# Issuing three stores and one small load from GpSimd instead of SyncE in a two-part state-space kernel

## The chip, the cores and the metric

The kernel runs on one core of a Trainium2 chip. The metric is the time of one execution on the device in microseconds (us); of several runs the median counts. The core has five engines that run side by side, each through its own list of instructions in order: TensorE (PE in the profile, with its weight loads as PEld), VectorE (DVE), ScalarE (ACT), GpSimd (POOL) and SyncE (SP). Data moves between the main memory (DRAM) and the on-chip memory by transfers (DMAs). A transfer is issued by an instruction of one of the engines; an instruction that waits, for data or for a transfer, holds up everything behind it on its engine.

## The reference

Two independent parts, over 2048 steps and 640 channels, are computed and set side by side. Part A is a diagonal linear recurrence with complex state (S5), part B a short convolution and a long one (H3). Cut to what matters:

```python
def part_a(x, Lambda, Bmat, Cmat, log_dt, Dskip):
    Lam_bar = exp(exp(log_dt) * Lambda)
    h[t] = Lam_bar * h[t - 1] + B_bar @ x[t]
    return 2 * real(Cmat @ h) + x * Dskip

def part_b(q, k, v, shift_k, ssm_k, ssm_D):
    k_shift = sum(k_pad[:, t:t + S] * shift_k[:, 3 - t] for t in range(4))
    kv = k_shift * v
    y = irfft(rfft(kv, 2 * S) * rfft(ssm_k, 2 * S))[:S]
    return q * (y + kv * ssm_D)

out = concatenate([part_a(...), part_b(...)], axis=-1)
```

Inputs and output are bf16. "D's row" below is `Dskip`, the 640 numbers that part A multiplies x by.

## The kernel before

All data lies in one on-chip array (`arena`), cut into named parts. `P.add` registers one operation with the engines that may run it, what it reads and what it writes; there are 815 of them. A hand-written table, `ORDER`, lists them as number, engine letter (T TensorE, V VectorE, A ScalarE, G GpSimd, S SyncE) and accumulator bank. `Program.emit` (L122) goes down the table and puts each operation at the end of its engine's list. It makes an operation wait for all that it depends on where that ran on another engine or is a transfer. So the table alone sets what stands behind what on each engine, and nearly all transfers stand in SyncE's list.

Part B takes k and v in five blocks of 128 channels (d = 0 to 4). For each block:

- `load_kv` (L811) loads k and v turned by the transfer (channels on partitions), L814. There is one buffer for k, so the k of the next block can only be issued when the last tap of this block has read it. For v there are three.
- `conv` (L827) makes four taps (`cm`, a multiplication by one weight per channel; its instructions are recorded under L205 on VectorE and L206 on ScalarE), three additions (`ca`, L840), and the product with v (`cx`, L841), which stays in v's buffer.
- `plane` (L843) stores the product, 128 x 2048, as 128 rows of `kv_rows`, a scratch tensor in DRAM (`pl`, L847). 

The stored rows come back in another layout by `relay` (L850): eight transfers per half (`rl`, L857), which need the rows of blocks 0 to 2 for the first half. TensorE then runs the long convolution in stages (`s1` L876 and L881, `s2` L900, `r2` L951, `r1` L972). What they leave in the accumulator is moved out by ScalarE or VectorE at L886, L913, L956 and L990. The filter `ssm_k` is loaded per half by four transfers (`load_h`, L807), to which VectorE adds the direct term (L809).

Part A builds its state by matmuls (L581, L602), a scan over the coarse steps (`coarse`, L656, whose products L679 and sums L690 run on VectorE) and a way back down (L728). Its last stage, `project` (L732), has 16 pieces: load 128 rows of x (L736), multiply them by D's row (`xd`, L737), project the state by TensorE (`C`, recorded under L225, or L229 where `wide` splits a matmul in two), add both (`ev_C`, L754) and store (L765). D's row is loaded once, spread over 128 partitions, by `ld_Dr` (L372). The x rows of the turned kind (L547) and C (`load_C`, L556) are loaded by SyncE too.

In the table of before, the three stores of blocks 0 to 2 (operations 388, 399 and 410) and D's row (91) are SyncE's. The first store stands behind the load of block 2's k, the second behind the load of C's imaginary part and ahead of block 3's k, the third behind the first relay. D's row stands behind the second half's `ssm_k`.

Of the kernel before, what the change touches and what calls it, by code (L numbers as in the profile page):

```python
# [20 lines left out]
PACT, PDVE, PPOOL, PPE, PSP = "A", "V", "G", "T", "S"  # L21
# [177 lines left out]
class Ctx:  # L199
# [9 lines left out]
    def v(self, name, lo=0, n=None):  # L209
        at, size = LAY.at[name]  # L210
        n = size - lo if n is None else n
        assert lo + n <= size
        return self.arena[:, at + lo:at + lo + n]
# [18 lines left out]
def bc(ap, shape):  # L232
    return ap.to_broadcast(shape)
# [124 lines left out]
def params(c):  # L358

    P, nc, v, f = c.P, c.nc, c.v, c.f  # L360
    V, G, A = PDVE, PPOOL, PACT
    lam_re, lam_im, ldt_in, dsk_in = c.ins["A_Lambda_re"], c.ins["A_Lambda_im"], c.ins["A_log_dt"], c.ins["A_Dskip"]
# [3 lines left out]
    for k, src in enumerate((lam_re, lam_im, ldt_in)):  # L366
        rows = pr[10 * k:10 * k + 10, :]
        P.add("ld_par", {PSP: .1, PACT: .1}, lambda e, rows=rows, src=src: e.dma_start(
            out=rows.rearrange("p (a b) -> p a b", a=2), in_=bass.AP(src.tensor, 0, [[64, 10], [0, 2], [1, 64]])),
            outs=[tk[:, k:k + 1]], ins=[pr], nbytes=2560)  # L370
    c.DR = v("DR")
    P.add("ld_Dr", {PSP: .1}, lambda e: e.dma_start(out=c.DR, in_=bass.AP(dsk_in.tensor, 0, [[0, 128], [1, 640]])), outs=[c.DR],  # L372
          nbytes=128 * 1280)
    PV = v("PV").bitcast(f32)
    g = P.group(1)
# [11 lines left out]
    for i, n in enumerate((1, 2, 4, 8, 16)):  # L387
        P.add("rn", {A: .2}, lambda e, i=i, n=n: e.activation(out=rn[:, i, :], in_=rho, func=FN.Exp, scale=float(n)),
              outs=[rn[:, i, :]], ins=[rho])
# [17 lines left out]
    for i in range(1, 4):  # L407
        P.add("fn", {G: .2}, lambda e, i=i: e.tensor_tensor(out=fn[:, i, :], in0=fn[:, i - 1, :], in1=fn[:, i - 1, :], op=ALU.add),
              outs=[fn[:, i, :]], ins=[fn[:, i - 1, :]])
    P.add("ph", {G: .4}, lambda e: e.tensor_tensor(  # L410
        out=ph.rearrange("p (x m) -> p x m", m=2), in0=bc(fn.rearrange("p n j -> p (n j)").rearrange("p (x o) -> p x o", o=1), [128, 40, 2]),
# [5 lines left out]
        out=al3, in0=al3, in1=bc(rn[:, 0:4, :].rearrange("p n j -> p (n j)").rearrange("p (x o) -> p x o", o=1), [128, 40, 2]), op=ALU.mult),  # L417
        outs=[al], ins=[al, rn[:, 0:4, :]])
# [4 lines left out]
    for lo, mi, val in ((0, 0, 1.0), (0, 1, 0.0), (64, 0, 0.0), (64, 1, 1.0)):  # L423
# [17 lines left out]
          outs=[t3(ga)[:, :, 0]], ins=[t3(ma)[:, :, 0], t3(mb)[:, :, 1]])  # L441
    P.add("ga1", {V: .12}, lambda e: e.tensor_tensor(out=t3(ga)[:, :, 1], in0=t3(mb)[:, :, 0], in1=t3(ma)[:, :, 1], op=ALU.subtract),
          outs=[t3(ga)[:, :, 1]], ins=[t3(mb)[:, :, 0], t3(ma)[:, :, 1]])
# [26 lines left out]
    for x in range(2):  # L470
        ps, pc, jx = phs[:, 640 * x:640 * x + 640], phc[:, 640 * x:640 * x + 640], Fi[:, 5 * x:5 * x + 5]
        P.add("sph", {G: 1.2}, lambda e, ps=ps, jx=jx: e.tensor_tensor(
            out=ps.rearrange("p (j s) -> p j s", j=5), in0=bc(s16.rearrange("p (o s) -> p o s", o=1), [128, 5, 128]),
            in1=bc(jx.rearrange("p (j o) -> p j o", o=1), [128, 5, 128]), op=ALU.mult), outs=[ps], ins=[s16, jx])
        P.add("cph", {G: 1.2}, lambda e, ps=ps, pc=pc: e.tensor_tensor(out=pc, in0=ps, in1=bc(c30, [128, 640]), op=ALU.add),
              outs=[pc], ins=[ps, c30])
# [291 lines left out]
class PartB:  # L768
# [74 lines left out]
    def plane(self, d):  # L843

        c, P = self.c, self.c.P
        vt, tok = c.v("VT", 2048 * (d % 3), 2048), c.tok[:, d:d + 1]
        P.add(f"pl{d}", {PSP: 1.6}, lambda e: e.dma_start(out=c.kvdram[128 * d:128 * d + 128, :], in_=vt), outs=[tok], ins=[vt],  # L847
              nbytes=128 * 4096)

    def relay(self, hf):  # L850
# [162 lines left out]
def build(c):  # L1013
# [5 lines left out]
    setup(c)  # L1019
    tables_G(c)  # L1020
    params(c)
    b.load_small()
    for k in range(3):
# [74 lines left out]
def plain_order(P):  # L1098
# [16 lines left out]


ORDER = (
# [40 lines left out]
)  # L1158


# [68 lines left out]
```

## Time and profile before

| what | value |
|---|---|
| runs of the program | 187.35, 187.96 and 188.18 us; median 187.96 |
| span of the profiled execution | 187.3 us, 7665 instructions |
| TensorE clock granted | full in all 40 slices |
| DMA: bytes moved | 30.15 MB, 161 GB/s on average |
| DMA: time of the queue that SyncE issues to (q1) | 86.7% of 16 engines' span |
| DMA: time of the other queues together (q8, q10, q14) | 1.8% |

The profile gives no total for the profiled execution apart from its span, 187.3 us; the fastest of the three runs took 187.35, so hardly anything of a run lies outside the span. A transfer shows up twice: as an instruction of the issuing engine's queue (SPq), whose duration is the issue, and by its landing, the time from the issue to when the data is there. GpSimd issues no transfer in this kernel.

### The profile page before, as it was taken

Reading aid. Unit: us, or ns where it says so; the run is one execution under the profiler, and the core shown is the slowest. Engines: PE = TensorE matmul, PEld = TensorE weight load, DVE = VectorE, ACT = ScalarE, POOL = GpSimd, SP = SyncE. Lnnn points to the kernel's source line nnn. Section 1 sums busy time; section 2 is a strip of 40 time slices with the busy share of each in tenths; the row PEclk is TensorE's granted clock in tenths of the full one; section 3 lists DMA queues with packets and bytes.
Section 4 is the critical chain, followed back from the end, with each engine's and each line's share of the span. In section 5 each row is a group of like instructions: output and inputs, shape, how many; then the busy total and the mean of one; then the engine's idle time right before and its main releaser. Section 6 shows DMA issues by size and latency. Waiting matters only on the chain.

```text
span 187.3 us, 7665 instructions
## 1 busy us (share of the span) xinstructions
PE 175.6 (94%) x3398; PEld 126.3 (67%) x3399; DVE 158.0 (84%) x225; ACT 147.7 (79%) x181; POOL 72.6 (39%) x68
## 2 busy tenths in 40 slices
PE   7998999999799979979997999999999999999992
PEld 2565666677468756656685688776588876887770
DVE  3537964679959899999969999899999999998961
ACT  2469699989899979999997997997898883985000
POOL 8679999900000000008803925730740000551620
PEclk9999999999999999999999999999999999999999
DMA  5999999799999989999989479402496993058996
GB/s 153 191 184 158 200 143 140 141 174 182 198 253 154 290 179 152 180 182 154 138 109 251 154 170 133 75 5 72 122 196 120 210 227 85 15 160 187 208 219 173
DMA packets 106682, 30.15 MB, mean 161 GB/s; under 512 B 101274, under 2 KB 106010, under 8 KB 106650
## 3 DMA queue, kind: packets, MB, share of 16 engines
q1 hardware_dynamic: 106332, 29.35, 86.7%
q8 instruction: 26, 0.43, 1.1%
q10 hardware_dynamic: 318, 0.33, 0.6%
q14 instruction: 6, 0.05, 0.1%
HBM read 11.32 MB, written 7.86 MB: 102 GB/s over the span
## 4 chain that ended last, share of the span: by engine, by line
PE 54%; DVE 23%; DMA 9%; ACT 8%; issue 3%; DVEq 0%; ACTq 0%
PE acc L225 17%; PE acc L581 13%; DMA arena<-in_B_k_dram 9%; PE acc L229 6%; DVE arena L728 6%; PE acc L900 6%; DVE arena L205 5%; ACT arena L913 5%; PE acc L951 4%; DVE arena L840 3%; PE acc L972 3%; PE acc L539 2%; DVE arena L754 2%; PE acc L881 1%; ACT arena L886 1%
## 5 line engine op out<-in xcount | busy, mean ns | idle before, releaser
L581 PE MATMUL acc<-arena 128*64 128x512 bf16 x400 | 45.6, 380 | 1.8 <-DVE arena L457 1.1
L913 ACT CAST arena<-acc 128x960 bf16<-128x960 f32 (+1 forms) x43 | 37.4, 916 | 4.0 <-PE acc L900 2.2
L225 PE MATMUL acc<-arena 128*128 128x320 bf16 (+2 forms) x255 | 36.4, 297 | 2.2 <-DVE arena L754 1.1
L581 PEld LDWEIGHTS <-arena 128*64 128x64 bf16 x400 | 26.0, 110 | 17.8 <-DVE arena L457 1.3
L886 ACT CAST arena<-acc 128x1024 bf16<-128x1024 f32 x37 | 35.8, 1034 | 2.1 <-PE acc L881 2.0
L225 PEld LDWEIGHTS <-arena 128*128 128x128 bf16 x256 | 23.7, 98 | 12.1 <-DVE arena L754 1.3
L841 POOL TENSOR_TENSOR arena<-arena 128x2048 bf16<-128x2048 bf16 x2 | 8.8, 4410 | 53.7 <-DVE arena L840 46.1
L900 PE MATMUL acc<-arena 128*64 128x160 bf16 x512 | 23.6, 235 | 1.8 <-DVE arena L679 1.4
L900 PEld LDWEIGHTS <-arena 128*64 128x64 bf16 x512 | 18.6, 110 | 8.3 <-ACT arena L913 2.2
L229 PE MATMUL acc<-arena 128*64 128x320 bf16 (+3 forms) x258 | 23.2, 313 | 0.5 <-DVE arena L690 0.5
L840 DVE TENSOR_TENSOR arena<-arena 128x2048 bf16<-128x2048 bf16 x14 | 17.6, 1256 | 4.5 <-ACT arena L206 4.3
L728 DVE TENSOR_TENSOR arena<-acc,arena 128x1024 bf16<-128x1024 f32 (+2 forms) x19 | 20.4, 1114 | 0.9 <-PE acc L229 0.5
L760 POOL TENSOR_TENSOR arena<-arena 128x640 bf16<-128x640 f32 x3 | 4.2, 1416 | 32.6 <-ACT arena L752 32.6
L956 ACT CAST arena<-acc 128x1024 bf16<-128x1024 f32 x16 | 15.4, 1025 | 1.7 <-PE acc L951 1.6
L229 PEld LDWEIGHTS <-arena 128*64 128x64 bf16 x258 | 13.0, 110 | 3.5 <-DVE arena L690 0.6
L876 PE MATMUL acc<-arena 128*64 128x128 bf16 x400 | 14.6, 220 | 0.2 <-ACT arena L886 0.2
L876 PEld LDWEIGHTS <-arena 128*64 128x64 bf16 x400 | 12.9, 110 | 2.4 <-ACT arena L886 0.9
L205 DVE TENSOR_SCALAR arena<-arena 128x2048 bf16<-128x2048 bf16 x15 | 11.0, 749 | 3.6 <-DMA arena<-in_B_k_dram 3.5
L754 DVE TENSOR_TENSOR arena<-acc,arena 128x640 bf16<-128x640 f32 x13 | 10.7, 820 | 3.5 <-PE acc L225 2.2
L206 ACT ACTIVATE arena<-arena 128x2048 bf16<-128x2048 bf16 (+2 forms) x10 | 11.1, 1112 | 1.5 <-DMA arena<-in_B_k_dram 1.5
L924 DVE TENSOR_TENSOR arena<-arena 128x2560 bf16<-128x2560 bf16 x8 | 11.9, 1484 | 0.1
L602 PE MATMUL acc<-arena 128*64 128x256 bf16 (+2 forms) x140 | 11.6, 291 | 0.1
(142 smaller groups left out, 284.4 us busy)
## 6 DMA issues: line engine op xcount, KB each, us to landing
out_dram<-arena SPq DMA_DIRECT2D x32, 160.0 KB, 3.3
arena<-in_B_ssm_k_dram SPq DMA_DIRECT2D x8, 320.0 KB, 6.1
kv_rows<-arena SPq DMA_DIRECT2D x5, 512.0 KB, 4.7
arena<-kv_rows SPq DMA_DIRECT2D x16, 160.0 KB, 4.0
arena<-in_A_x_dram SPq DMA_DIRECT2D x16, 160.0 KB, 3.5
arena<-in_B_q_dram SPq DMA_DIRECT2D x8, 320.0 KB, 6.3
arena<-in_A_B_im_dram ACTq DMA_DIRECT2D x1, 160.0 KB, 2.8
arena<-in_A_B_re_dram SPq DMA_DIRECT2D x1, 160.0 KB, 3.0
```

What stands on the lines that cost most here:

```text
L205: vm = lambda e: lambda out, in_, by: e.tensor_scalar_mul(out=out, in0=in_, scalar1=by)
L225: e.matmul(out, lhsT=lhsT, rhs=rhs, start=start, stop=stop, skip_group_check=True)
L229: e.matmul(out[half], lhsT=lhsT[:, half], rhs=rhs, start=start, stop=stop, skip_group_check=True, tile_position=(0, 64 * r))
L581: e.matmul(o[64 * r:64 * r + 64], lhsT=self.BT[j][:, r, d, :], rhs=self.XP[:, d, 2 * q:2 * q + 2], start=(d == 0), stop=(d == 4), skip_gro ...
L728: e.tensor_tensor(out=o, in0=b, in1=o, op=ALU.add)
L754: e.tensor_tensor(out=two(ys), in0=two(B)[:, :, 0:320], in1=two(ys), op=ALU.add)
L840: P.add(f"ca{d}_{j}", tt, lambda e: e.tensor_tensor(out=t1, in0=t1, in1=t2, op=ALU.add), outs=[t1], ins=[t1, t2])
L876: e.matmul(B[64 * b:64 * b + 64, 128 * i:128 * i + 128], lhsT=lh[i], rhs=F[:, b, :], start=True, stop=True, tile_position=(0, 64 * b))
L886: P.add(f"e1{what}{hf}_{u}", {PACT: act(1024), PDVE: dve(1024)}, lambda e, B: c.CP[e](out=out, in_=(B.rearrange("p (l n s k) -> p k s l n" ...
L900: e.matmul(B[64 * s:64 * s + 64, 512 * b + 160 * i:512 * b + 160 * i + 160], lhsT=c.W[:, k, 64 * b:64 * b + 64], rhs=self.AS[hf][:, k, 160 ...
L913: c.CP[e](out=out, in_=b.rearrange("p r (k j n) -> p r k j n", k=n, j=4) if nj > 1 else b.rearrange("p r (k x) -> p r k x", k=n))
L956: P.add(f"er2{hf}_{u}", {PACT: act(1024), PDVE: dve(1024)}, lambda e, B: c.CP[e](out=out, in_=B.rearrange("p (s n b) -> p b s n", s=2, n=4 ...
```

## The change

The three stores and D's row may now be run by GpSimd, and the table gives them to it. Each store stands in the table right behind the product that it stores (operations 387, 398 and 409, all on VectorE), and D's row right behind the first store. The order of all other operations is as it was. The stores of blocks 3 and 4 stay SyncE's.

```diff
-    P.add("ld_Dr", {PSP: .1}, lambda e: e.dma_start(out=c.DR, in_=bass.AP(dsk_in.tensor, 0, [[0, 128], [1, 640]])), outs=[c.DR],
+    P.add("ld_Dr", {PSP: .1, PPOOL: .1}, lambda e: e.dma_start(out=c.DR, in_=bass.AP(dsk_in.tensor, 0, [[0, 128], [1, 640]])), outs=[c.DR],
...
-        P.add(f"pl{d}", {PSP: 1.6}, lambda e: e.dma_start(out=c.kvdram[128 * d:128 * d + 128, :], in_=vt), outs=[tok], ins=[vt],
+        P.add(f"pl{d}", {PSP: 1.6, PPOOL: 1.6}, lambda e: e.dma_start(out=c.kvdram[128 * d:128 * d + 128, :], in_=vt), outs=[tok], ins=[vt],
...
-    "57A0 84G0 387V0 201T4 154A0 177S0 195T6 245T0 196A6 202V4 390S0 226A2 391V0 392V0 191T2 246A0 136V0 229T4 393V0 269S0 "
+    "386V0 79G0 75A0 389S0 262V6 238A0 225T2 150G0 254A4 188V0 176S0 57A0 84G0 387V0 388G0 91G0 201T4 154A0 177S0 195T6 245T0 196A6 "
```

SyncE's list around the loads of k and v of blocks 2 and 3, with what went (-) and came (+). `in_B_k` and `in_B_v` are the loads of k and v, `in_A_C_im` is C's imaginary part, `kv_rows<-arena` are the stores and `arena<-kv_rows` the relays:

```order
 L814 DMA_TRANSPOSE arena<-in_B_k_dram 128x2048
-L847 DMA kv_rows<-arena 128x2048
 L814 DMA_TRANSPOSE arena<-in_B_v_dram 128x2048
 L556 DMA_TRANSPOSE arena<-in_A_C_im_dram 128x4x640
-L847 DMA kv_rows<-arena 128x2048
 L814 DMA_TRANSPOSE arena<-in_B_k_dram 128x2048
-L857 DMA arena<-kv_rows 32x40x64
-L847 DMA kv_rows<-arena 128x2048
-L857 DMA arena<-kv_rows 32x40x64
+L857 DMA arena<-kv_rows 32x40x64 x2
 L795 DMA arena<-in_B_ssm_D_dram 4x80
 L857 DMA arena<-kv_rows 32x40x64 x4
```

The three stores are gone from between the loads, so that the load of block 3's k follows C's imaginary part directly; the relays keep their order. Further down SyncE's list, behind the second half's filter (`in_B_ssm_k`):

```order
 L736 DMA arena<-in_A_x_dram 128x640
 L807 DMA arena<-in_B_ssm_k_dram 32x80x64 x4
-L372 DMA arena<-in_A_Dskip_dram 128x640
 L736 DMA arena<-in_A_x_dram 128x640
 L814 DMA_TRANSPOSE arena<-in_B_v_dram 128x2048
```

D's row is gone from there, and a load of x follows the filter. GpSimd's list behind its work on the tables (L475 and L350) and ahead of block 3's product (L841):

```order
 L475 TENSOR_TENSOR arena<-arena 128x640
 L350 TENSOR_TENSOR arena<-arena 128x512
+L847 DMA kv_rows<-arena 128x2048
+L372 DMA arena<-in_A_Dskip_dram 128x640
+L847 DMA kv_rows<-arena 128x2048 x2
 L841 TENSOR_TENSOR arena<-arena 128x2048
 L840 TENSOR_TENSOR arena<-arena 128x2048
```

The four issues stand together there, between two pieces of GpSimd's own work. The lists of TensorE, VectorE and ScalarE are unchanged.

76 rows, old and new, of the table ORDER are left out of this document.

## The prediction

> **What bounds the kernel now.** I read the page's busy times first, then TensorE's own rows for where it waits, and from there back: the rows of VectorE, of SyncE's queue and of GpSimd around those places.
>
> ```profile
> PE 175.6 (94%) x3398; PEld 126.3 (67%) x3399; DVE 158.0 (84%) x225; ACT 147.7 (79%) x181; POOL 72.6 (39%) x68
> ```
>
> TensorE (PE) is busy for 175.6 of 187.3 us, in a fixed order. So the change can win only what stands in PE's gaps, 11.7 us in all. Its longest one behind the first moved store is this (the bracket gives the idle time ahead of a row and what ended it):
>
> ```profile
> 67.41 0.61 PE L900 MATMUL acc<-arena 128*64 128x160 bf16 x12 [1.39 <-DVE arena L679]
> ```
>
> VectorE (DVE) was late there, and its rows tell why:
>
> ```profile
> 37.89 1.23 DVE L841 TENSOR_TENSOR arena<-arena 128x2048 bf16<-128x2048 bf16 x1 [1.83 <-DMA arena<-in_B_v_dram]
> ...
> 50.83 1.23 DVE L841 TENSOR_TENSOR arena<-arena 128x2048 bf16<-128x2048 bf16 x1
> 53.96 0.75 DVE L205 TENSOR_SCALAR arena<-arena 128x2048 bf16<-128x2048 bf16 x1 [1.90 <-DMA arena<-in_B_k_dram]
> ...
> 58.84 0.75 DVE L205 TENSOR_SCALAR arena<-arena 128x2048 bf16<-128x2048 bf16 x1
> ...
> 61.51 1.22 DVE L841 TENSOR_TENSOR arena<-arena 128x2048 bf16<-128x2048 bf16 x1
> ...
> 65.20 1.42 DVE L205 TENSOR_SCALAR arena<-arena 128x2048 bf16<-128x2048 bf16 x2 [0.65 <-DMA arena<-in_B_k_dram]
> ```
>
> The rows of L841 are the products of blocks 0, 1 and 2; they end at 39.12, 52.06 and 62.73. L205 are the taps, which need their block's k. DVE waits 1.90 for block 2's k and 0.65 for block 3's; right behind block 3's first taps, which end at 66.62, it does the L679 that PE waits for until 67.41.
>
> The next gap has another cause. DVE stands still for D's row, and PE behind it:
>
> ```profile
> 95.96 0.53 DVE L809 TENSOR_TENSOR arena<-arena 128x80 bf16<-128x80 bf16 x1
> 97.87 0.49 DVE L737 TENSOR_TENSOR arena<-arena 128x640 bf16<-128x640 bf16 x1 [1.38 <-DMA arena<-in_A_Dskip_dram]
> 98.49 0.82 DVE L754 TENSOR_TENSOR arena<-acc,arena 128x640 bf16<-128x640 f32 x1
> ```
> ```profile
> 94.59 2.88 PE L229 MATMUL acc<-arena 128*64 128x320 bf16 x40
> 97.40 1.00 PE L881 MATMUL acc<-arena 64*64 64x64 bf16 x96
> 99.37 2.89 PE L225 MATMUL acc<-arena 128*128 128x320 bf16 x20 [0.97 <-DVE arena L754]
> ```
>
> SyncE's queue (SP), which issues all these transfers, has one right behind the other:
>
> ```profile
> 41.39 3.49 SPq L814 DMA_TRANSPOSE arena<-in_B_v_dram  x1
> 44.97 3.10 SPq L556 DMA_TRANSPOSE arena<-in_A_C_re_dram  x1
> 48.18 2.14 SPq L814 DMA_TRANSPOSE arena<-in_B_k_dram  x1
> 50.37 0.58 SPq L847 DMA_DIRECT2D kv_rows<-arena  x1
> ...
> 54.97 3.23 SPq L556 DMA_TRANSPOSE arena<-in_A_C_im_dram  x1
> 58.30 1.40 SPq L847 DMA_DIRECT2D kv_rows<-arena  x1
> 59.81 3.06 SPq L814 DMA_TRANSPOSE arena<-in_B_k_dram  x1
> ...
> 63.59 0.63 SPq L847 DMA_DIRECT2D kv_rows<-arena  x1
> ...
> 90.58 3.45 SPq L372 DMA_DIRECT2D arena<-in_A_Dskip_dram  x1
> ```
>
> The stores (L847) leave at 50.37, 58.30 and 63.59: 11.3, 6.2 and 0.9 us behind their products.
>
> **The change, part by part.** The four issues go to GpSimd (POOL), which has nothing to do then:
>
> ```profile
> 84.01 4.08 POOL L841 TENSOR_TENSOR arena<-arena 128x2048 bf16<-128x2048 bf16 x1 [46.12 <-DVE arena L840]
> ```
>
> POOL idles 46.12 us, from 37.9 to 84.0. The issues wait for products that end at 39.12, 52.06 and 62.73, so behind the last there are 21 us before L841, the next work queued there. What an issue costs on POOL no row shows; the bounds are the 0.58 us of the first store on SP and those 21 us. I take nothing, since it lies in idle time. If that cover went, L841 would be late, us for us.
>
> *Term 1, D's row.* Today it is issued at 90.58, behind the four loads of the filter's second half. Issued at about 40 it has 56 us to land. DVE then runs L737 right behind L809, at 96.49. What is late next is TensorE's first output projection (PE's L229 above), whose sum L754 reads: it ends at 97.47. So L754 runs from 97.5 to 98.3 instead of from 98.49 to 99.31, and the next projection can follow L881 at 98.40: the whole gap of 0.97 goes. The DVE work behind cannot all move as far, since some of it waits for ScalarE, which gets nothing from this; so I book **0.9** (bounds 0 and 0.97, and it is near the upper one because PE and DVE both stand still there today).
>
> *Term 2, the wait for block 3's k.* SP issues this load when block 2's last tap is done (58.84 + 0.75 = 59.59), so its issue cannot come earlier. What goes is the second store, issued 1.5 us ahead of it. Ahead of block 2's and block 3's k stands a load of C each; the times from their issues, at 44.97 and 54.97, to landing are:
>
> ```profile
> DMA to landing us min/median/max: 5.8/5.8/5.8
> ```
> ```profile
> DMA to landing us min/median/max: 6.5/6.5/6.5
> ```
>
> The first landed at 50.8, and block 2's k, directly behind it, at 53.9 (DVE goes on at 53.96): 3.1 us later. The second landed at 61.5. With no store between, block 3's k should land at 61.5 + 3.1 = 64.6, not just before 65.20. DVE is through with its other work at 65.20 - 0.65 = 64.55. So nearly the whole 0.65 goes, and PE's gap at 67.41 shrinks by as much.
>
> *Term 3, what the early transfers take from block 2's k.* Store 0 and D's row now move while v1, C and k2 are loaded. The sizes (and a relay's, for below), and the rate with which bytes move over 40 to 48 us and while a store is in flight (the last number is GB/s):
>
> ```profile
> kv_rows<-arena SPq DMA_DIRECT2D x5, 512.0 KB, 4.7
> arena<-kv_rows SPq DMA_DIRECT2D x16, 160.0 KB, 4.0
> ```
> ```profile
> arena<-in_A_Dskip_dram SPq DMA_DIRECT2D x1, 160.0 KB
> ```
> ```profile
> 40.00:48.00 8.00, 6.97 (x101) 4.89 (x96) 7.00 (x10) 7.31 (x9) 0.00 (x0) 1.00 1.06 170
> ```
> ```profile
> 60.50:62.50 2.00, 2.00 (x36) 1.39 (x32) 2.00 (x3) 1.80 (x5) 0.00 (x0) 1.00 1.08 348
> ```
>
> Store and row are 672 KB, at 348 GB/s 2.0 us. If they fit into what the loads leave free (348 - 170 GB/s over 8 us is 1.4 MB, twice the need), k2 is not late at all; if the loads stand still meanwhile, it is 2.0 us late. Between these I go by SP's issues: the v load of 41.39 took 3.49, the equally large k load of 48.18 only 2.14. So the queue was held up for 1.35 of the 6.7 us from 41.39 to 48.07, a fifth, and I let a fifth of the 2.0 us show: **0.4 late**. DVE waits for k2 already (1.90), so this passes on in full, to block 2's taps and so to the issue of block 3's k too: DVE would be free for block 3 at 64.95 instead of 65.20. Terms 2 and 3 together give 0.65 - 0.4 = **0.25**.
>
> [...]
>
> *Later moves.* SP is relieved of four issues, and what follows on it can only come sooner. POOL's order is otherwise the same. Between 67 and 97 PE, DVE and ScalarE wait for one another, so they shift together.
>
> The sum is 0.9 + 0.25 = 1.15 us off the profiled execution, whose span is 187.3 us. The median of the runs, 187.96, lies 0.6 above that span; taken off the median, the forecast is **186.8**.
>
> **The rivals.** *Full cover:* store and row fit into the room, k2 is not late: 0.65 + 0.97 = 1.6 off, 186.3. The 1.4 MB speak for it, SP's held issues against it.
>
> *The stores eat the gain:* k2 is 1.5 late, most of the 2.0; PE's gap at 67.41 grows by 0.85, D's row gives 0.9 back: 187.9. The change then brings the stores forward and the loads back.
>
> *Slower, by a collision:* each store starts while the next block's k is under way: store 1 from 52.06, k2 landing at 53.9. If they take turns on the engines, store 0 and the row cost k2 2.0 us and store 1 up to 512 KB at 348 GB/s, 1.5, more. k2 is then 3.5 late; less 0.65 and 0.9 that is 1.9 to 2.0 slower, 189.9. It decides from k2 being 1.55 late, and shows as slower from 2.5. Against it: GpSimd must get its transfer going first, and k2 is nearly through by then.
>
> [...]
>
> **How the numbers follow.** Forecast, 186.8: 0.46. Full cover, 186.3: 0.13. Gain eaten, 187.9: 0.20. Collision, 189.9, and what lies on the way to it: 0.14. Held up, 187.1: 0.07. The runs of before scatter by 0.8 us, and about 0.5% (0.94 us, so 187.0) is what a measurement of this kernel can tell from no change. Faster by more: 0.33 of the forecast's 0.46, full cover, and 0.02 of held up: 0.48. Slower by more: the collision and 0.02 of gain eaten: 0.16. Within: 0.36. The range, 186.0 to 188.7, leaves out little but the collision's far end: its low end is full cover less a third of the scatter, its high end k2 2.3 us late.
>
> **What would show it.** Right: no DVE wait for D's row and no gap ahead of PE's L225 at 98.4; DVE's wait before block 3's taps near nothing; the bracket at block 2's first tap about 2.3 instead of 1.90; L841 on POOL no later. Wrong: over 3.4 in that bracket, or a gap ahead of PE's L900 longer than 1.39; a PE wait for the relays at L876; or a new gap right behind the one that D's row closes, which would mean that another engine was due there anyway.

## The result, and the profile after

| | before | changed |
|---|---|---|
| runs | 187.35, 187.96, 188.18, 190.49 us | 192.77, 193.50, 193.52, 193.63 us |
| median | 188.07 us | 193.51 us |
| ratio | | 1.0284 (95% interval 1.0253 to 1.0315) |

The changed kernel is slower by 5.4 us; the prediction was 186.8 (186.0 to 188.7). Ratios, here and below, leave out executions far above the fastest one of the same kernel; since such executions turn out to be part of this change's effect, medians and spreads are given beside them.

The page of the changed kernel (an execution of 192.77 us), its span, its busy times and the TensorE clock in 40 slices:

```profile
span 191.0 us, 7669 instructions
PE 177.9 (93%) x3398; PEld 127.2 (67%) x3399; DVE 158.5 (83%) x225; ACT 147.5 (77%) x181; POOL 76.8 (40%) x72
PEclk9999999999999957999999999999999999999999
```

The clock row has a 5 and a 7 now, at 67 to 76 us; before, it was full throughout. VectorE's rows around block 2 (start, duration; the bracket is the idle time ahead and what ended it), the same as shown of before:

```profile
48.62 1.23 DVE L841 TENSOR_TENSOR arena<-arena 128x2048 bf16<-128x2048 bf16 x1
55.81 0.75 DVE L205 TENSOR_SCALAR arena<-arena 128x2048 bf16<-128x2048 bf16 x1 [5.97 <-DMA arena<-in_B_k_dram]
...
66.33 0.74 DVE L205 TENSOR_SCALAR arena<-arena 128x2048 bf16<-128x2048 bf16 x1
```

DVE waits 5.97 us for block 2's k instead of 1.90. The wait for block 3's k (0.65) is gone. TensorE's rows at the place of the long gap, and the windows behind it (length, busy time of each engine, granted clock, DMA share, GB/s):

```profile
64.19 0.61 PE L900 MATMUL acc<-arena 128*64 128x160 bf16 x12
68.52 1.01 PE L900 MATMUL acc<-arena 128*64 128x160 bf16 x12 [3.73 <-DVE arena L679]
...
71.34 3.84 PE L581 MATMUL acc<-arena 128*64 128x512 bf16 x20
```
```profile
68.00:70.00 2.00, 1.48 (x20) 1.48 (x22) 2.00 (x4) 0.00 (x1) 0.00 (x0) 0.50 0.23 90
70.00:72.00 2.00, 2.00 (x28) 1.71 (x26) 2.00 (x3) 1.58 (x3) 0.00 (x0) 0.50 0.69 109
72.00:74.00 2.00, 2.00 (x12) 0.83 (x10) 1.93 (x3) 1.57 (x2) 0.00 (x0) 0.50 1.29 156
74.00:76.00 2.00, 2.00 (x32) 1.44 (x30) 0.00 (x0) 0.33 (x1) 0.00 (x0) 0.90 1.40 138
```

The gap is 3.73 instead of 1.39, and behind it TensorE runs at half its clock until about 74: the 20 matmuls of L581 take 3.84, where they took 2.33 before. At the place of D's row, DVE waits only for TensorE, and TensorE goes on from L881 to L225 without a gap:

```profile
101.48 0.82 DVE L754 TENSOR_TENSOR arena<-acc,arena 128x640 bf16<-128x640 f32 x1 [0.79 <-PE acc L229]
```
```profile
101.31 1.00 PE L881 MATMUL acc<-arena 64*64 64x64 bf16 x96
102.36 1.80 PE L225 MATMUL acc<-arena 128*128 128x320 bf16 x12
```

GpSimd's issues and the work queued behind them, then SyncE's queue:

```profile
38.73 1.07 POOL L847 DMA_DIRECT2D kv_rows<-arena  x1
39.81 0.66 POOL L372 DMA_DIRECT2D arena<-in_A_Dskip_dram  x1
50.14 0.54 POOL L847 DMA_DIRECT2D kv_rows<-arena  x1 [9.67 <-DVE arena L841]
64.89 0.54 POOL L847 DMA_DIRECT2D kv_rows<-arena  x1 [14.21 <-DVE arena L841]
87.86 4.08 POOL L841 TENSOR_TENSOR arena<-arena 128x2048 bf16<-128x2048 bf16 x1 [22.44 <-DVE arena L840]
```
```profile
39.30 6.31 SPq L814 DMA_TRANSPOSE arena<-in_B_v_dram  x1
45.71 3.37 SPq L556 DMA_TRANSPOSE arena<-in_A_C_re_dram  x1
49.19 3.10 SPq L814 DMA_TRANSPOSE arena<-in_B_k_dram  x1
```

The issues cost GpSimd 0.5 to 1.1 us each, in idle time, as assumed. But the load of block 1's v, behind store 0, now holds SyncE's queue for 6.31 us (3.49 before).

### The profile page after: what moved, and what is told of

Read it like the earlier page. It is cut to its first block, busy times and chain, and to the rows that moved or that the text cites. A ratio compares the mean times of both kernels' runs of the same rounds, so it can differ in the third digit from the quotient of the medians.

```text
span 191.0 us, 7669 instructions
## 1 busy us (share of the span) xinstructions
PE 177.9 (93%) x3398; PEld 127.2 (67%) x3399; DVE 158.5 (83%) x225; ACT 147.5 (77%) x181; POOL 76.8 (40%) x72
## 3 DMA queue, kind: packets, MB, share of 16 engines
q1 hardware_dynamic: 105756, 27.61, 81.8%
q0 software_dynamic: 480, 1.74, 2.5%
## 4 chain that ended last, share of the span: by engine, by line
PE 27%; DVE 24%; DMA 16%; POOL 11%; ACT 8%; SPq 6%; issue 4%; DVEq 0%; POOLq 0%; ACTq 0%
PE acc L225 12%; DMA arena<-in_B_v_dram 7%; PE acc L229 5%; DVE arena L728 4%; PE acc L900 4%; POOL arena L309 4%; DMA arena<-in_B_k_dram 3%; SPq L807 3%; PE acc L951 3%; DVE arena L840 3%; DVE arena L205 3%; DMA arena<-in_A_x_dram 3%; DMA kv_rows<-arena 3%; DVE arena L924 2%; ACT arena L913 2%
## 5 line engine op out<-in xcount | busy, mean ns | idle before, releaser
L581 PE MATMUL acc<-arena 128*64 128x512 bf16 x400 | 47.1, 389 | 0.5 <-DMA arena<-in_A_B_im_dram 0.3
L581 PEld LDWEIGHTS <-arena 128*64 128x64 bf16 x400 | 25.8, 113 | 18.2 <-issue 2.9
L225 PE MATMUL acc<-arena 128*128 128x320 bf16 (+2 forms) x255 | 36.2, 297 | 1.2 <-ACT arena L886 0.8
L225 PEld LDWEIGHTS <-arena 128*128 128x128 bf16 x256 | 23.7, 98 | 10.9 <-ACT arena L575 0.7
L900 PE MATMUL acc<-arena 128*64 128x160 bf16 x512 | 24.8, 243 | 4.1 <-DVE arena L679 3.7
L900 PEld LDWEIGHTS <-arena 128*64 128x64 bf16 x512 | 19.7, 114 | 10.6 <-DVE arena L679 3.9
L841 POOL TENSOR_TENSOR arena<-arena 128x2048 bf16<-128x2048 bf16 x2 | 9.3, 4668 | 28.8 <-DVE arena L840 28.8
L229 PEld LDWEIGHTS <-arena 128*64 128x64 bf16 x258 | 13.0, 110 | 3.8 <-DVE arena L690 0.6
L876 PEld LDWEIGHTS <-arena 128*64 128x64 bf16 x400 | 12.8, 110 | 2.4 <-ACT arena L886 0.8
L350 POOL TENSOR_TENSOR arena<-arena 128x512 int32<-128x512 int32 x8 | 12.0, 1511 | 0.1
```

The costliest lines, as they stand in the source:

```text
L225: e.matmul(out, lhsT=lhsT, rhs=rhs, start=start, stop=stop, skip_group_check=True)
L229: e.matmul(out[half], lhsT=lhsT[:, half], rhs=rhs, start=start, stop=stop, skip_group_check=True, tile_position=(0, 64 * r))
L581: e.matmul(o[64 * r:64 * r + 64], lhsT=self.BT[j][:, r, d, :], rhs=self.XP[:, d, 2 * q:2 * q + 2], start=(d == 0), stop=(d == 4), skip_gro ...
L876: e.matmul(B[64 * b:64 * b + 64, 128 * i:128 * i + 128], lhsT=lh[i], rhs=F[:, b, :], start=True, stop=True, tile_position=(0, 64 * b))
L900: e.matmul(B[64 * s:64 * s + 64, 512 * b + 160 * i:512 * b + 160 * i + 160], lhsT=c.W[:, k, 64 * b:64 * b + 64], rhs=self.AS[hf][:, k, 160 ...
```

## The experiments

Numbers in the diffs are the table's: 387, 398, 409 are the products of blocks 0, 1, 2; 388, 399, 410 their stores; 91 is D's row; 390 the load of block 1's v; 391, 392 and 402 taps of VectorE; 439 to 442 the second half's filter; 729 the second load of x; 311 TensorE's L900 behind the gap; 322 VectorE's scan L684. All medians of before below (186.66 to 187.01) are from the same chips as the runs they are compared with.

**An ordinary execution of before.** The kernel unchanged, for a second profile.

> The kernel before itself, for a second profile of it. If the profiled execution on which the prediction was built was an ordinary one, this one shows its gaps again: about 1.4 us ahead of L900 near 67 us, and DVE's waits for block 0's v (1.83) and block 1's k (0.90). If it was an unusually late one, the span is 184 to 185.5 us, those two waits are gone and the gap ahead of L900 is below 0.6 us, so that there was hardly anything to win there.

It took 187.09 us, at a span of 185.3. So 1.8 us lie outside the span, and the execution on which the prediction was built, with its span of 187.3, must have taken about 189.1: it was a late one. Its waits for block 0's v and block 1's k are hardly there in this one (0.26, none), and TensorE's gap ahead of L900 is 0.24. DVE's wait for block 2's k, and three places of TensorE by which executions can be lined up:

```profile
52.27 0.75 DVE L205 TENSOR_SCALAR arena<-arena 128x2048 bf16<-128x2048 bf16 x1 [2.09 <-DMA arena<-in_B_k_dram]
```
```profile
65.07 0.60 PE L900 MATMUL acc<-arena 128*64 128x160 bf16 x12 [0.24 <-DVE arena L679]
77.80 0.22 PE L225 MATMUL acc<-arena 128*128 128x128 bf16 x1 [0.81 <-ACT arena L886]
...
126.69 3.32 PE L225 MATMUL acc<-arena 128*128 128x320 bf16 x22 [0.15 <-DVE arena L754]
```

The same places in the changed kernel:

```profile
83.99 0.22 PE L225 MATMUL acc<-arena 128*128 128x128 bf16 x1 [0.79 <-ACT arena L886]
...
131.71 3.32 PE L225 MATMUL acc<-arena 128*128 128x320 bf16 x22 [0.15 <-DVE arena L754]
```

This gives the account of the 5.7 us between the spans (191.0 and 185.3). L900 starts 3.45 later (68.52 and 65.07). From there to the first L225 it takes 15.47 instead of 12.73: 2.74 for the lowered clock. From there to the last row it takes 47.72 instead of 48.89: 1.17 given back where D's row was waited for. The rest takes 59.29 instead of 58.61: 0.68 more, in the last third, which I didn't follow up.

**The parts apart.** Only D's row on GpSimd:

```diff
-    ... 387V0 201T4 ... 439S0 ... 91S0 ...
+    ... 387V0 91G0 201T4 ... 439S0 ...
```

> Only D's row goes to GpSimd, at the place it has in the changed kernel; the three stores stay SyncE's. Theory: the loss has three parts, namely about 1.8 us outside the span as soon as GpSimd issues any transfer, block 2's k coming late because store 0 stops SyncE's loads, and TensorE's halved clock behind the long gap; the row gives 0.95 back. Then here: span 186.4 (187.3 - 0.95), time 188.2, TensorE's gap ahead of L900 about 1.4, clock full. Rival: it is the row, not the store, that stops the loads: gap above 2.5, clock halved, span above 189. Rival on the part outside the span: it grows with each GpSimd transfer, so a quarter of 1.8 here, time 186.9.

187.66 us (186.4 to 189.51), 1.0046 of before (1.0014 to 1.0078). The row gains nothing here: VectorE waits 1.24 us for the filter at the place where it used to wait for the row, and block 2's k is 0.5 late (its first tap starts at 52.77 instead of 52.27). Only the three stores:

```diff
-    ... 387V0 201T4 ... 398V0 ... 409V0 ...
+    ... 387V0 388G0 201T4 ... 398V0 399G0 ... 409V0 410G0 ...
```

> Only the three stores go to GpSimd; D's row stays where it was on SyncE. Theory: span 191 to 192 (the changed kernel's 191.0 plus 0.95, less what the row added to the delay of block 2's k), outside the span 1.8, time 193 to 194; TensorE's gap ahead of L900 3 to 3.7 and its clock at half behind it. Rival, the row is to blame: gap below 2, clock full, span 187.5 to 188.5.

190.92 us (188.71 to 191.8), 1.0144 (1.0085 to 1.0204). The stores alone cost half of the change's 2.8% by these ratios, and 4.3 of its 5.4 us by the medians. In the execution that was profiled, store 0 left 2.53 us ahead of block 1's v and k was not late (1.92); there the clock fell further on, behind two short gaps of 1.26 and 0.57 at 98 and 100 us. D's row early, but by SyncE, ahead of the filter:

```diff
-    ... 729S0 ... 439S0 ... 91S0 ...
+    ... 729S0 91S0 ... 439S0 ...
```

> No GpSimd transfer: SyncE issues D's row ahead of the four loads of the filter's second half instead of behind them; all else as before. Theory: VectorE's wait of 1.38 for the row and TensorE's gap of 0.97 go, time 187.0 to 187.2 against 188.0, and what lies outside the span is as in the kernel before. Rival: the gap is filled by another wait (ScalarE's), time within 0.3 of before.

187.84 us (187.29 to 190.98), 1.0054 (1.0027 to 1.0081): no gain. VectorE has no wait for D's row, but one right ahead of it, for the filter:

```profile
95.67 0.52 DVE L809 TENSOR_TENSOR arena<-arena 128x80 bf16<-128x80 bf16 x1 [1.64 <-DMA arena<-in_B_ssm_k_dram]
```

Its time lies 1.75 above its span, and GpSimd issues nothing; so the 1.8 outside the span are no price of GpSimd's queue. With the filter brought forward as well:

```diff
-    ... 335V0 ... 729S0 ... 440S0 ... 441S0 ... 442S0 ... 439S0 ... 91S0 ...
+    ... 335V0 440S0 441S0 442S0 439S0 91S0 ... 729S0 ...
```

> No GpSimd; SyncE loads the second half's filter and D's row ahead of the second load of x instead of behind it, so the filter leaves about 1.2 us sooner than in the run with the row early. If D's row early gained nothing because DVE then waited for the filter (1.64 us there), that wait falls to about 0.4, TensorE's gap ahead of L881 goes, and the time is 0.995 to 1.0 of the kernel before. If another engine is due there anyway (the stages behind 97 us hold the end), it is 1.0 to 1.006, as with the row early alone.

186.91 us (185.91 to 191.03), 1.0011 (0.9974 to 1.0047). Both waits are gone, and the stretch from the first to the last L225 is 1.08 shorter than in before (77.93 to 125.74); but the rest then takes 59.16 instead of 58.61, and the time is the same. This was the best version found; it doesn't beat the kernel before by anything that can be measured.

**Stores held back, or early by SyncE.** Store 0, D's row and store 1 held on GpSimd until block 2's first tap:

```diff
+    for op in (388, 91, 399):
+        c.P.ops[op].preds.add(402)
```

> As the changed kernel, but store 0, D's row and store 1 are issued by GpSimd only when VectorE has made block 2's first tap, so when block 2's k has landed; store 2 as in the changed kernel. Theory (store 0 takes the engines from the loads ahead of block 2's k): VectorE's wait at block 2's first tap back at about 1.9, TensorE's gap ahead of L900 at most 2, clock full, span 186.4 to 187.5, time 188.2 to 189.3 because the 1.8 outside the span stay. Rival (GpSimd transfers hurt wherever they stand): the gap stays above 3, the clock halves, span about 191.

188.63 us (187.49 to 191.58), 1.0089 (1.0057 to 1.0121). Block 2's k is on time (2.17), now block 3's is late (2.15); a gap of 2.08 ahead of L900, the clock full behind it. With store 0 and D's row left to SyncE as in the kernel before, store 2 on GpSimd as in the changed one, and store 1 on GpSimd held in this way:

```diff
+    c.P.ops[399].preds.add(402)
```

> Store 0 and D's row as before (SyncE); stores 1 and 2 by GpSimd, store 1 held until block 2's first tap has run, so that it cannot stand in the way of block 2's k. If the harm is done by what moves ahead of block 2's k, it is gone: DVE's wait for block 2's k as in the kernel before, no long gap ahead of L900, and the time is 0.994 to 1.003 of the kernel before (the gain of block 3's k, at most 0.65 us). If store 1 now does to block 3's k what store 0 did to block 2's, DVE waits for block 3's k by 1 to 3 us, and the time is 1.005 to 1.015. If any transfer by GpSimd has a price of its own, 1.01 or more without either wait.

187.75 us (186.41 to 196.6), 1.0038 (1.0005 to 1.0072): DVE waits 0.89 for block 3's k, TensorE's gap is 1.54, with no dip. Then the same early place without GpSimd: SyncE issues store 0 and D's row right behind block 1's v.

```diff
-    ... 390S0 ... 400S0 ... 388S0 ... 91S0 ...
+    ... 390S0 388S0 91S0 ... 400S0 ...
```

> GpSimd issues nothing. SyncE itself issues store 0 and D's row right behind the load of block 1's v, so their bytes stand in SyncE's queue about where GpSimd's stood in time, ahead of block 2's k; stores 1 and 2 stay where they were. If it is the bytes ahead of block 2's k that cost, whoever issues them, DVE waits for block 2's k about 4 to 6 us, TensorE's gap ahead of L900 is about 3 us or more, and the time is 3 to 6 us above the kernel before (1.015 to 1.03). If it is GpSimd's queue that stops SyncE's turned loads, k is late by only about 2 us (672 KB at 348 GB/s), the gap is 1 to 2 us, and the time is within 1.01 of the kernel before.

189.34 us (188.57 to 190.17), 1.0138 (1.01 to 1.0176).

```profile
54.36 0.75 DVE L205 TENSOR_SCALAR arena<-arena 128x2048 bf16<-128x2048 bf16 x1 [4.20 <-DMA arena<-in_B_k_dram]
```

The wait is 4.20 instead of 2.09: k is 2.1 later, as much as 672 KB take at 348 GB/s (2.0). So in this run, in SyncE's own queue, the bytes ahead of k cost in full. TensorE's gap is 2.12, the clock full behind it. In the changed kernel's first profile k was 3.5 late (55.81 instead of 52.27, though product 0 had ended 0.2 earlier), so something came on top there. Most of that lateness was there before store 1 left at 50.14: k's own issue started at 49.19 instead of 46.12, which is 3.07 late.

**What the gap does to the clock.** First, the changed kernel again, and with idle matmuls (whose result nobody reads) in the place of the gap, ahead of 311:

```diff
+    def keep(e, B):
+        for r in range(24):
+            e.matmul(B, lhsT=c.I3[:, 0:128], rhs=W2[:, 0:512], start=True, stop=True)
```

> The changed kernel once more, beside the next three on one chip. All theories: 5 to 6 us above the kernel before (1.025 to 1.031); a granted clock below full behind TensorE's gap ahead of L900, and block 2's k as the reason of that gap.

> The changed kernel with 24 idle matmuls of 128x512 (about 2.8 us) put in TensorE's list in the place of the gap ahead of L900; their result is read by nobody. If the dip of the granted clock behind that gap is caused by the gap, the clock stays at 1.0 there, the L581 behind it takes 2.3 us instead of 3.8, and the time falls by 1.5 to 2.5 us against the changed kernel, to about 1.015 of the kernel before. If the dip has another cause (the transfers, or the time in the program), it stays and the time is that of the changed kernel or above.

The changed kernel took 186.79, 187.86, 190.83 and 194.7 us here, beside 186.66 of before: it can be as fast. The profiled execution is the fastest of the four; DVE waits 1.75 for k, and there is no gap. The filled kernel, 197.31 us, 1.0571 (1.052 to 1.0621), is a miss: 23 of the idle matmuls took 5.13 us, not 2.8, and its execution had k on time (2.66). So the question was put to the kernel before, without a change to any transfer:

```diff
     c.P.depend()
+    c.P.ops[311].preds.add(322)
```

> The kernel before, no transfer changed; TensorE's L900 at the place of the long gap waits for one more VectorE operation (the scan L684, some 3.6 us behind the L679 it waits for anyway), which opens a gap of about 3.5 us. If a long gap by itself lowers TensorE's clock, the granted clock is 0.98 to 0.99 on average with a stretch at 0.5 behind the gap, and the time is the kernel before plus the gap plus 2 to 3.4 us: 191.5 to 193.5. If the dip in the changed kernel came from its transfers, the clock stays at 0.995 or above and the time is 189.5 to 190.5.

192.27 us (191.39 to 192.8), 1.0267 (1.021 to 1.0324).

```profile
69.26 1.01 PE L900 MATMUL acc<-arena 128*64 128x160 bf16 x12 [3.72 <-DVE arena L684]
```
```profile
70.00:72.00 2.00, 2.00 (x32) 2.00 (x30) 1.07 (x2) 1.23 (x2) 0.00 (x0) 0.50 1.25 152
```

A gap of 3.72 us alone, with all transfers as before, was enough for a clock of 0.50 behind it, and cost nearly what the change costs. And the same wait with 12 of the idle matmuls in the gap:

```diff
+        for r in range(12):
```

> The same forced wait, with 12 idle matmuls of 128x512 (0.22 us each, about 2.7 us, read by nobody) in TensorE's list in the gap. What waits for what is otherwise as in the run before, so the work resumes at the same time. If the idle time lowers the clock, the clock stays at 0.995 or above here and the time is 2 to 3 us below the run with the open gap. If idle time isn't the cause, the two are equal.

192.92 us (192.67 to 198.06), 1.0288 (1.0233 to 1.0342). The clock stayed full in all 40 slices, and from L900 (67.87) to the first L225 (80.56) it took 12.69 instead of 13.95 (69.26 to 83.21): the dip cost 1.26 there. But the total isn't lower, because TensorE then stops elsewhere for nothing that the profile shows, 1.58 and 2.08 us:

```profile
101.99 1.25 PE L225 MATMUL acc<-arena 128*128 128x320 bf16 x8 [1.58 <-issue]
```

So the cause of the dip is shown by the clock and by the stretch behind the gap, not by the total.

**What makes block 2's k so late.** In the late execution store 0 left 0.57 us ahead of block 1's v, in the one without a gap 1.22 behind it. Two kernels force the order: v held until a tap behind product 0, and store 0 held until two taps behind it.

```diff
+    c.P.ops[390].preds.add(391)
```
```diff
+    c.P.ops[388].preds.add(392)
```

> The changed kernel with the load of block 1's v held on SyncE until the first tap behind product 0 has run, so that GpSimd's store 0 always leaves ahead of it. If that order makes block 2's k late, every execution is like the slow one of the changed kernel: DVE's wait for block 2's k 4 us or more, the gap ahead of L900 3 us or more, the granted clock 0.99 or below, 191 to 194 us. If the order doesn't decide, the times spread as those of the changed kernel do (187 to 194 us).

> The changed kernel with store 0 (and D's row behind it) held on GpSimd until two taps behind product 0 have run, about 2.2 us later, so that the load of block 1's v leaves first. If the order decides, every execution is like the fast one of the changed kernel: wait for block 2's k about 2 us, hardly a gap ahead of L900, clock 0.995 or above, 186.5 to 188 us. If it is the bytes ahead of block 2's k whatever their order, the wait is 3.5 to 6 us and the times are 189 to 194 us.

> The changed kernel beside the two before, for its spread on this chip: all theories 186.8 to 194 us. Where its profiled execution has a gap of over 3 us ahead of L900, the granted clock dips behind it; where the gap is below 2.2 us, it doesn't.

Store first: 187.7 us (186.82 to 188.11), 1.0019 (0.9964 to 1.0074). v first: 192.9 us (189.75 to 193.98), 1.0192 (1.0098 to 1.0287). The changed kernel beside them: 193.09 us (191.11 to 195.52), 1.0278 (1.0197 to 1.0359). The order matters, but the other way round than I expected. The rows of the changed kernel here, SyncE's and GpSimd's, the landing of store 0, VectorE's waits for block 1's v and block 2's k, and the windows of 44 to 50 us (last number: GB/s):

```profile
38.72 3.51 SPq L814 DMA_TRANSPOSE arena<-in_B_v_dram  x1
42.33 8.62 SPq L556 DMA_TRANSPOSE arena<-in_A_C_re_dram  x1
51.05 3.75 SPq L814 DMA_TRANSPOSE arena<-in_B_k_dram  x1
```
```profile
38.79 1.14 POOL L847 DMA_DIRECT2D kv_rows<-arena  x1
```
```profile
DMA to landing us min/median/max: 11.5/11.5/11.5
```
```profile
51.16 1.22 DVE L841 TENSOR_TENSOR arena<-arena 128x2048 bf16<-128x2048 bf16 x1 [2.45 <-DMA arena<-in_B_v_dram]
59.61 0.76 DVE L205 TENSOR_SCALAR arena<-arena 128x2048 bf16<-128x2048 bf16 x1 [7.22 <-DMA arena<-in_B_k_dram]
```
```profile
44.00:46.00 2.00, 2.00 (x26) 1.32 (x24) 2.00 (x4) 1.98 (x3) 0.00 (x0) 1.00 1.27 138
46.00:48.00 2.00, 2.00 (x46) 1.59 (x42) 2.00 (x4) 1.95 (x3) 0.00 (x0) 1.00 1.24 110
48.00:50.00 2.00, 2.00 (x45) 1.51 (x44) 0.71 (x1) 1.95 (x4) 0.00 (x0) 1.00 1.00 163
```

And of the kernel with the store first:

```profile
40.07 4.39 SPq L814 DMA_TRANSPOSE arena<-in_B_v_dram  x1
44.55 2.92 SPq L556 DMA_TRANSPOSE arena<-in_A_C_re_dram  x1
47.58 2.90 SPq L814 DMA_TRANSPOSE arena<-in_B_k_dram  x1
```
```profile
DMA to landing us min/median/max: 5.4/5.4/5.4
```
```profile
42.00:44.00 2.00, 2.00 (x22) 1.27 (x19) 1.97 (x2) 2.00 (x3) 0.00 (x0) 1.00 1.14 412
44.00:46.00 2.00, 2.00 (x23) 1.32 (x21) 1.97 (x3) 2.00 (x2) 0.00 (x0) 1.00 1.18 266
```

With the store first, it has landed at 44.2, at the end of a window of 412 GB/s, and the loads behind it go on at 193 GB/s and more. Where store and v leave together, the windows from 42 to 50 us show 110 to 163 GB/s, store 0 takes 11.5 us to land, VectorE waits 2.45 for v itself (until 51.16), and k's issue slips to 51.05. The first profile of the changed kernel lies between: 386 GB/s from 42 to 44, then 124 to 184. In numbers, of the profiled executions, with the mean rate in one window from 38 to 50 us:

| kernel | store 0 ahead of v by | landing | GB/s, 38 to 50 us | wait for block 2's k | gap ahead of L900 | clock, mean | time |
|---|---|---|---|---|---|---|---|
| store first | 1.26 | 5.4 | 218 | 2.47 | 0.27 | 0.998 | 188.11 |
| changed, first profile | 0.57 | 7.0 | 193 | 5.97 | 3.73 | 0.981 | 192.77 |
| changed, third | -0.07 | 11.5 | 145 | 7.22 | 7.29 | 0.980 | 195.52 |
| changed, second | -1.22 | 6.5 | 230 | 1.75 | none | 0.998 | 186.79 |
| v first | -2.87 | 4.6 | 185 | 6.97 | 6.21 | 0.979 | 193.98 |

The ordinary execution of before, without the early transfers, has 194 GB/s in the same 12 us. Its window, then that of the changed kernel's first profile and that of the store first:

```profile
38.00:50.00 12.00, 12.00 (x195) 8.56 (x189) 11.81 (x15) 11.31 (x14) 0.99 (x1) 1.00 1.09 194
```
```profile
38.00:50.00 12.00, 12.00 (x194) 8.53 (x188) 11.70 (x14) 11.26 (x14) 2.47 (x3) 1.00 1.11 193
```
```profile
38.00:50.00 12.00, 12.00 (x175) 8.55 (x170) 11.86 (x14) 11.26 (x14) 2.16 (x3) 1.00 1.17 218
```

So in the first profile the 672 KB brought no more bytes per second, and the loads gave way to them: at 194 GB/s they are an estimated 3.5 us, which is what k was late. In the third the rate fell as well, and k was 7.3 late (59.61 instead of 52.27). Where k was on time, the rate had risen, to 218 and 230, and to 231 in the kernel with the stores alone.

In the kernel with v first, store 0 is quick, but D's row and C stay side by side (9.5 and 10.6 us to landing): 130 and 106 GB/s from 46 to 50, and the issue of k takes 5.94 us instead of 2.90; store 1 left at 51.11, during that issue, and its part there wasn't separated. The changed kernel's second execution shows that v first can also go well (338 and 263 GB/s from 44 to 48); why it did stays open.

## Why the prediction was wrong

**Term 3 (k2 0.4 late) failed, and with it the sum.** I took the transfers to share a rate that adds up to 348 GB/s, "a fifth of the 2.0 us". The upper bound, 2.0, didn't hold: in the changed kernel's first profile k was 3.5 late, in the third 7.3, and inside SyncE's own queue the loads lose all of the 2.0 (2.1). The 348 GB/s of one window of 2 us wasn't the rate of the stretch: from 38 to 50 us the mean stayed at 193 (194 in before), and in the third profile it fell to 145. The two lines that I took the room from have a hint against it: their DMA share is 1.06 at 170 GB/s and 1.08 at 348, so by that column the transfer engines were as busy at half the rate. The room was used only in some executions. The one kernel that was fast in all four of its executions has the store 1.26 us ahead of v; there k was 0.39 late (52.66), about the 0.4 of term 3. The collision rival had the lateness of the first profile (3.5) by luck: it put 1.5 of it to store 1, and 3.07 were there before store 1 left. Something of the kind shows in the kernels with stores held, at block 3's k (waits of 2.15 and 0.89).

**A term was missing: the clock.** Behind the gaps of 3.73 and 3.72 us in TensorE the granted clock was 0.50, which cost 2.74 here and 1.26 in the kernel with the gap alone. I priced a wait at its own length. In the profiles the clock dipped behind the single gaps of 3.42 to 7.29 us and stayed full behind those of 1.54, 2.08 and 2.12. The length of one gap doesn't decide it, though: in the kernel with the stores alone the clock fell behind gaps of 1.26 and 0.57 (0.57 from 100 to 102 us).

**Term 1 (D's row, 0.9) was right in the changed kernel and not elsewhere.** There 1.17 came back. Where the rest wasn't delayed, the wait for the filter took the row's place (1.24 with the row alone on GpSimd, 1.64 with the row early by SyncE), much as the last of the signs that I had named against it. **Term 2** (block 3's k no longer behind store 1) isn't shown by any run: the wait is gone in the changed kernel, but an ordinary execution of before has no wait for block 3's k either, and a gap of only 0.24, so there was nothing to gain.

**The base was off.** I read the span as nearly the whole time. 1.8 us lie outside it, so the profiled execution was one of 189.1 us, later than the three times shown, and the gaps that the terms were to win were partly its own.

**GpSimd's side was right:** issues of 0.5 to 1.1 us in idle time, and none of them delayed until VectorE's taps end. The 0.07 for "held up" was for a store 2 that GpSimd issues only when VectorE's taps have ended, which was my supposition and is shown by no run: in the changed kernel store 2 left at 64.89, while the tap of 66.33 was still to come.

What stays open: why store 0 and the turned load of C took so long side by side (11.5 and 12.7 us to landing in the third profile, 5.4 and 6.3 with the store first), and what lets two of the twelve executions of the changed kernel escape it (186.79 and 187.86). The page of the changed kernel lists GpSimd's transfers on a queue of another kind (q0, software_dynamic, 1.74 MB; SyncE's q1, 27.61 MB, is hardware_dynamic). Whether that kind of queue matters behind the issue, or any second queue would do the same, no run shows; the same transfers issued by ScalarE would tell. VectorE being busy doesn't decide it: it was as busy from 38 to 50 us with the store first (11.86 us) as in the first profile (11.70).

## What to carry to other kernels

The transfers that moved to another engine's queue weren't out of the way of the loads here: with 672 KB, which are 2.0 us at the 348 GB/s of one window, moved ahead, block 2's k was 3.5 and 7.3 us later where store 0 left 0.57 ahead of block 1's v and 0.07 behind it, and 0.39 later where it was made to leave 1.26 ahead. Before moving a transfer forward, name the next load that the slowest engine waits for, and keep the transfer behind it, or well ahead and in one piece. Where TensorE's work waits, price a long gap with the lowered clock behind it (here 2.74 and 1.26 us on top of gaps of 3.73 and 3.72), and check by a second profile whether the gap that is to be won is there in ordinary executions.

## What the hardware did that was not expected

- In three profiles of the same program, the changed kernel, store 0 took 6.5, 7.0 and 11.5 us to land, with 230, 193 and 145 GB/s on average from 38 to 50 us; the times were 186.79, 192.77 and 195.52 us.
- The granted clock fell to 0.50 at TensorE's gaps of 3.72, 3.73 and 7.29 us, for some 3.4, 6.8 and 6.8 us by the windows of 2 us; with the gap of 6.21 the mean clock of the execution was 0.979. It also fell behind a stop of 3.42 us at 158.5 us in the kernel with 24 idle matmuls (40 matmuls of L225 took 7.28 us there, 5.61 at 187.25; mean clock 0.991). What a gap cost on top of its length was about half of the low time that was left behind it: some 5.7 us in the first profile of the changed kernel (2.74 lost), 2.8 in the kernel with the gap alone (1.26 lost). It stayed at 1.00 behind gaps of 2.08 and 2.12, and fell once behind 1.83 us of idling in two pieces.
- In both kernels with idle matmuls put into TensorE's list, TensorE stopped later at places where the profile names no cause (up to 3.42 us with 24 of them, 1.58 and 2.08 with 12); in the second profile of before the longest such stop was 0.38, in the other kernels 0.94. That the idle matmuls cause these stops isn't shown, but in neither kernel did filling the gap make the time shorter.
